# Cosine and sine products of a Fourier stage kept in separate PSUM halves, with three shared two-bank PSUM slots and mixing over whole batches

## The chip, the cores and the metric

One core of a Trainium2 chip runs the whole program. The metric is the device time of one execution in microseconds. The kernel before took 491.13, 491.68 and 493.02 us.

## The reference

The input x has 8 batches of 3072 positions of 256 channels, in f32. Two steps follow each other:

```python
X = np.fft.fft(np.fft.fft(x, axis=1), axis=2)
x = X.real                                      # (8, 3072, 256)
x_prev = x shifted by one position (first row 0)
xk = mu_k * x + (1 - mu_k) * x_prev
xr = mu_r * x + (1 - mu_r) * x_prev
k = max(xk @ w_k, 0)                            # 256 -> 1024
v = (k * k) @ w_v                               # 1024 -> 256
out = sigmoid(xr @ w_r) * v
```

## The kernel before, in words

**The Fourier part** works on one batch at a time and splits the 3072 positions into 48 x 64. It needs only real arithmetic on half of the channel pairs and half of the positions, since the real part of the result is symmetric. A GpSimd DMA loads a half batch as f16 (tile `xh`, line 101), VectorE forms sum and difference of the channel halves (`butterfly`, line 114, tile `eo`), and three kinds of matmul items follow on TensorE:
- **A items** (line 364, tile `psA`): 4 matmuls of 96 columns each, the Fourier sum over 48. ScalarE copies the result to tile `a` as f16.
- **D items** (line 397, tile `psD`): 4 matmuls of 128 columns for two units of work, the Fourier sum over the channels; ScalarE copies into `g_all`, a ring of 10 units of 384 columns.
- **C items** (lines 413, 415, 416, tile `psC`): the last sequence stage. For each of 27 slices, three matmuls with different weights: cosine table `m1` against 128 columns that are the same table twice (line 413), sine table `m2` with both signs side by side (128 columns, line 415), and `m1` once more for the second half only (64 columns, line 416). All three accumulate in PSUM, so that the two halves of a slice leave PSUM as finished rows, and ScalarE copies them to `y`.

For batch 0, `a_first` (line 381) does the butterfly inside the matmuls: two accumulating matmuls of 96 columns for each sum and each difference.

**The mixing** (`mix`, lines 456, 462, 473) is on VectorE: differences of neighbouring slices `d`, `t = mu * d` and `x = y + t` (or minus), for 8 slices at a time. The half m = 1 is the mirrored one, written backwards.

**The network part** is cut in 48 chunks of 512 positions (8 batches x 3 pieces x 2 halves) and each chunk in 4 steps. Step n has one K piece (4 matmuls of 512 columns, line 488, into a two-bank tile `psK`), its relu on ScalarE (line 492), its square on VectorE every second step (line 497), and, 5 steps late (`LAG`), one V tile (8 matmuls of 256 columns, line 518, tile `psV`). Every two steps four matmuls of line 506 make `psR`, ScalarE takes the sigmoid (line 510), VectorE multiplies (line 525), and SyncE's queue writes the output.

**PSUM** has 8 banks: `psK` two tiles of two banks, `psV` two of one bank, and `psF`, shared by the A, D, C and R items, two of one bank.

**The order** is written by hand: `work` holds for each half step the items to issue between the matmuls, and `pin_order` fixes each engine's instructions in program order. An engine that waits holds up all that stands behind it. Ahead of step 0 the program builds its tables, and batch 0 goes through A, D and C, with matmuls on zeros (`keep_busy`, line 136) in between.

## Time and profile before

| | |
|---|---|
| Median of three runs | 491.68 us (491.13 to 493.02) |
| The profiled execution's own time | 490.52 us |
| Span of its trace, first to last instruction | 488.4 us |
| Time outside the span | 2.1 us |
| TensorE busy | 469.4 us (96%) |
| ScalarE busy | 383.3 us (78%) |
| VectorE busy | 366.8 us (75%) |
| Mean granted clock of TensorE | 0.988 |

In the profile PE is TensorE's matmuls, PEld its weight loads, DVE VectorE, ACT ScalarE, POOL GpSimd and SP SyncE. A group of rows names the line of the program, the engine, the operation, what is written from what, the shape, the count, and the busy time with the mean of one in ns. Matmuls overlap each other: the mean of one is the time from its start to its last result, and what one costs in a stream is the distance between the starts of two neighbours. A row of windows names a stretch of the span, then its length and each engine's busy time in it, and TensorE's granted clock, where 1.00 is full speed.

### The profile page before, as it was taken

How to read it: one execution, taken by the hardware profiler on the slowest of the kernel's cores; microseconds unless marked ns; L12 is line 12 of the kernel's file. 1: busy time of each engine (PE TensorE's matmuls, PEld its weight loads, DVE VectorE, ACT ScalarE, POOL GpSimd, SP SyncE). 2: the span in 40 equal slices, each digit the busy share in tenths (PEclk: the TensorE clock that was granted, in tenths of full speed). 3: DMA queues.
4: the chain of work that ended last, by engine and by line, in shares of the span. 5: the costliest groups of instructions: out<-in, count | busy, mean ns of one | idle time of the engine just before them, and what ended most of it. 6: DMA issues, size and time to landing. Idle time of an engine off the chain costs nothing.

```text
span 488.4 us, 10652 instructions
## 1 busy us (share of the span) xinstructions
PE 469.4 (96%) x4325; PEld 345.5 (71%) x4325; DVE 366.8 (75%) x614; ACT 383.3 (78%) x559; POOL 38.7 (8%) x64
## 2 busy tenths in 40 slices
PE   7879889999999999999999999999999999999996
...
PEclk9889989999999999999999999999999999999999
...
GB/s 141 53 196 109 112 104 107 99 77 64 111 125 50 66 127 47 125 51 65 126 82 97 46 96 93 50 66 54 57 56 55 65 51 59 58 57 74 72 67 87
DMA packets 32565, 40.28 MB, mean 82 GB/s; under 512 B 4164, under 2 KB 30276, under 8 KB 31172
## 3 DMA queue, kind: packets, MB, share of 16 engines
...
q14 instruction: 15, 0.12, 0.1%
...
## 4 chain that ended last, share of the span: by engine, by line
PE 85%; DVE 1%; ACT 1%; issue 0%; DVEq 0%
PE psV L518 32%; PE psK L488 31%; PE psR L506 8%; PE psD L397 4%; PE psA L364 4%; PE psC L413 2%; PE psC L415 2%; PE psC L416 1%; ACT rl L492 0%; DVE o L525 0%; DVE x L473 0%; DVE t L462 0%; DVE d L456 0%; ACT a L356 0%; DVEq L525 0%
## 5 line engine op out<-in xcount | busy, mean ns | idle before, releaser
L492 ACT ACTIVATE rl<-psK 128x1024 f16<-128x1024 f32 x192 | 196.2, 1022 | 34.1 <-PE psK L488 34.1
L488 PE MATMUL psK<-x,wk 128*128 128x512 f16 x768 | 218.5, 381 | 1.7 <-DVE x L473 1.1
L518 PE MATMUL psV<-wv_sb,k 128*128 128x256 f16 x1536 | 199.3, 273 | 0.0
L518 PEld LDWEIGHTS <-k 128*128 128x128 f16 x1536 | 150.6, 98 | 38.0 <-issue 0.5
L497 DVE TENSOR_TENSOR k<-rl 128x2048 f16<-128x2048 f16 x96 | 117.5, 1224 | 25.3 <-ACT rl L492 24.9
L525 DVE SCALAR_TENSOR_TENSOR o<-psV,r 128x512 f32<-128x512 f32 x96 | 66.3, 690 | 78.2 <-PE psV L518 62.8
L488 PEld LDWEIGHTS <-wk 128*128 128x128 f16 x768 | 62.3, 98 | 22.3 <-issue 3.4
L473 DVE TENSOR_TENSOR x<-y,t 128x1024 f16<-128x1024 f16 x96 | 66.5, 693 | 3.3
L356 ACT ACTIVATE g_all<-psD 128x512 f16<-128x512 f32 x90 | 53.4, 602 | 16.6 <-PE psD L397 10.1
L356 ACT ACTIVATE a<-psA 128x384 f16<-128x384 f32 x112 | 54.9, 490 | 14.1 <-PE psA L364 8.1
L510 ACT ACTIVATE r<-psR 128x512 f16<-128x512 f32 x96 | 57.3, 597 | 2.7 <-PE psR L506 2.7
L506 PE MATMUL psR<-wr,x 128*128 128x256 f16 x384 | 57.6, 272 | 0.0
L506 PEld LDWEIGHTS <-x 128*128 128x128 f16 x384 | 37.5, 98 | 24.8 <-issue 0.5
L356 ACT ACTIVATE y<-psC 128x512 f16<-128x512 f32 (+2 forms) x52 | 30.0, 577 | 19.3 <-PE psC L416 19.3
L364 PEld LDWEIGHTS <-eo 96*128 96x128 f16 x448 | 31.5, 98 | 18.9 <-DVE eo L114 4.1
L364 PE MATMUL psA<-w_a,eo 96*128 96x96 f16 x448 | 37.7, 206 | 3.8 <-DVE eo L114 3.8
L397 PEld LDWEIGHTS <-a 128*128 128x128 f16 x384 | 28.7, 98 | 14.2 <-issue 1.0
L101 POOL DMA_DIRECT2D xh<-in_x_dram x36 | 18.6, 525 | 246.9 <-DVE eo L114 245.6
L397 PE MATMUL psD<-w_eo,a 128*128 128x128 f16 x368 | 35.6, 220 | 0.2
L415 PE MATMUL psC<-m,g_all 128*128 128x128 f16 x208 | 34.3, 221 | 1.6 <-DVE m L300 1.6
L413 PE MATMUL psC<-m,g_all 128*128 128x128 f16 x208 | 34.3, 221 | 1.5 <-ACT g_all L356 0.8
L114 DVE TENSOR_TENSOR eo<-xh 96x2048 f16<-96x2048 f16 x28 | 34.0, 1214 | 0.0
...
## 6 DMA issues: line engine op xcount, KB each, us to landing
...
wk<-in_moe_w_k_dram,row_i POOLq DMA_INDIRECT x4
wr<-in_moe_w_r_dram,row_i POOLq DMA_INDIRECT x4
mu_f<-in_moe_mu_k_dram SPq DMA_DIRECT2D x1, 0.0 KB
```

The costliest lines, as they stand in the source:

```text
L356: nc.scalar.activation(out=out_ap, in_=in_ap, func=AF.Copy)
L364: nc.tensor.matmul(out=ps[:, 96 * i:96 * i + 96], lhsT=eo[:, 4 * grp + i, e, :], rhs=w_a[0:96], start=True, stop=True)
L397: nc.tensor.matmul(out=_v(ps, 256 * i + 64 * (1 - e), [(128, 2), (1, 64)]), lhsT=a_t[b][e][:, 2 * u:2 * u + 2, :], rhs=w_eo[:, e, :], star ...
L413: nc.tensor.matmul(out=o, lhsT=g[:, 128:256], rhs=_v(m1, 64 * sl, [(0, 2), (1, 64)]), start=True, stop=False)
L473: V.tensor_tensor(out=dst, in0=_v(y, 512 * i + 192 * m, [(64 * NSL, 2), (1, 512)]), in1=t, op=ALU.subtract if m else ALU.add)
L488: nc.tensor.matmul(out=st["kp"][:, 512 * hs:512 * hs + 512], lhsT=wk_sb[m][a][:, 128 * fc:128 * fc + 128], rhs=xk[:, a, m], start=(a == 0) ...
L492: nc.scalar.activation(out=st["rl"][:, 2 * ds:2 * ds + 2], in_=st["kp"].rearrange("p (f t) -> p f t", f=2), func=AF.Relu, bias=0.0, scale= ...
L497: V.tensor_tensor(out=k2_t[c][:, 2 * ds - 2:2 * ds + 2], in0=r, in1=r, op=ALU.mult)
L506: nc.tensor.matmul(out=ps[:, 256 * h:256 * h + 256], lhsT=x_t[b, i, 1][:, a, m, 128 * tb:128 * tb + 128], rhs=wr_sb[m][a], start=(a == 0), ...
L510: nc.scalar.activation(out=st["r"], in_=ps, func=AF.Sigmoid)
L518: nc.tensor.matmul(out=st["v"][:, 256 * h:256 * h + 256], lhsT=k2_t[c][:, fc, 128 * tb:128 * tb + 128], rhs=wv_sb[:, fc], start=(fc == 0), ...
L525: V.scalar_tensor_tensor(out=o.rearrange("p a b -> p (a b)"), in0=st["v"], scalar=16.0, in1=st["r"], op0=ALU.mult, op1=ALU.mult)
```

## The change

- **C items** write the cosine product P (one matmul of 64 columns) to one bank and the sine product Q (two accumulating matmuls of 64 columns, the second with the cosine table and the third block of weights) to the other bank of a two-bank tile. Both are copied to a tile `pq`. VectorE then makes the rows: `y` = P + Q and P - Q (`halves`). The table of the sine with the other sign and its making fall away. The tables of one column (slice 25) are swapped by three small VectorE instructions.
- **PSUM**: K pieces and A, D, C and R items all take a two-bank tile from three slots `psW` in turn; V keeps two one-bank slots. So A items have 8 matmuls, D items 8 (4 units), C items 7 slices, and R items a whole chunk of 512 positions, and each is copied in one ScalarE instruction. `g_all` holds all 24 units of a batch.
- **Mixing** goes over 24 slices at once: one difference for each half, `t` (`scaled`) and `x` (`mixed`) of 1536 elements. Tiles of the mixing, `y`, `a` and `pq` have one buffer each, `xh` and `eo` two in place of three.
- **Chunks** go by half m first, then by piece i. In a step the K piece comes whole, then the items, then the V tile; the square and the output product are issued at the end of a step.
- **Start**: batch 0 and the first half of batch 1 use `a_sum`: sum and difference side by side, two accumulating matmuls of 192 columns. 9 slices of the tables are made first, then 18. Before step 0 stand 9 slices of batch 0 (12 before), 12 matmuls on zeros inside the start (18 before), and batch 0's mixing of the next slices goes into steps 0 to 9.

```diff
-    xh_pool = ctx.enter_context(tc.tile_pool(name="xh", bufs=3))
-    eo_pool = ctx.enter_context(tc.tile_pool(name="eo", bufs=3))
-    a_pool = ctx.enter_context(tc.tile_pool(name="a_sb", bufs=1))
-    y_pool = ctx.enter_context(tc.tile_pool(name="y_sb", bufs=2))
-    mix_pool = ctx.enter_context(tc.tile_pool(name="mix", bufs=2))
+    xh_pool = ctx.enter_context(tc.tile_pool(name="xh", bufs=2))
+    eo_pool = ctx.enter_context(tc.tile_pool(name="eo", bufs=2))
+    y_pool = ctx.enter_context(tc.tile_pool(name="y_sb", bufs=1))
+    mix_pool = ctx.enter_context(tc.tile_pool(name="mix", bufs=1))
-    psum = ctx.enter_context(tc.tile_pool(name="psum", bufs=8, space=bass.MemoryType.PSUM))
-    def ps_k():
-        return psum.tile([P, 1024], FP32, name="psK", tag="psK", bufs=2)
+    ps_n = {"W": 0, "V": 0}
+    def ps_slot(kind, n, cols):
+        k = ps_n[kind] % n
+        ps_n[kind] += 1
+        return psum.tile([P, cols], FP32, name=f"ps{kind}{k}", tag=f"ps{kind}{k}", bufs=1)
+    def ps_w():
+        return ps_slot("W", 3, 1024)
     def ps_v():
-        return psum.tile([P, 512], FP32, name="psV", tag="psV", bufs=2)
-    def ps_f(name):
-        return psum.tile([P, 512], FP32, name=name, tag="psF", bufs=2)
+        return ps_slot("V", 2, 512)
...
-        ps = ps_t("psA", wide)
+        ps = ps_w()
+        for i in range(8):
+            nc.tensor.matmul(out=ps[:, 128 * i:128 * i + 96], lhsT=eo[:, 8 * j + i, e, :],
+                             rhs=w_pm[0:96, 0], start=True, stop=True)
+        evac(_v(a_t[b], 3072 * e + 2 * (16 * h + 8 * j), [(64, 48), (2, 8), (1, 2)]),
+             _v(ps, 0, [(2, 48), (128, 8), (1, 2)]), eng)
+    def a_sum(b, h, q0, eng="A"):
+        if (h, q0) == (0, 0):
+            a_tile(b)
+        xh = xh_t[b, h]
+        ps = ps_w()
         for i in range(4):
-            nc.tensor.matmul(out=ps[:, 96 * i:96 * i + 96],
-                             lhsT=eo[:, 4 * grp + i, e, :], rhs=w_a[0:96],
-                             start=True, stop=True)
-        src = _v(ps, 0, [(2, 48), (96, 4), (1, 2)])
-        dst = _v(a_t[b][e], 8 * (4 * h + grp), [(64, 48), (2, 4), (1, 2)])
-        evac(dst, src, eng)
...
-    def d_item(b, up, eng="A", wide=False):
-        ps = ps_t("psD", wide)
-        for i in range(2):
-            u = 2 * up + i
+    def d_item(b, n, eng="A"):
+        ps = ps_w()
+        for i in range(4):
+            u = 4 * n + i
             for e in range(2):
                 nc.tensor.matmul(out=_v(ps, 256 * i + 64 * (1 - e), [(128, 2), (1, 64)]),
-        evac(g_of(2 * up)[:, :, 1:257], ps.rearrange("p (i c) -> p i c", i=2), eng)
+        for h in range(len(eng)):
+            c = 4 // len(eng)
+            evac(g_all[:, 4 * n + c * h:4 * n + c * h + c, 1:257],
+                 ps[:, 256 * c * h:256 * c * (h + 1)].rearrange("p (i c) -> p i c", c=256),
...
+    def c_item(b, s0, n, eng="A"):
+        if s0 == 0:
-        n = min(4, NSL - 4 * grp)
+            y_t[b, "pq"] = y_pool.tile([P, 2, NSL, 64], FP16, name="pq")
+        pq = y_t[b, "pq"]
+        ps = ps_w()
-            g = g_of(u)[:, u % 2]
-            o = ps[:, 128 * i:128 * i + 128]
-            nc.tensor.matmul(out=o, lhsT=g[:, 128:256],
-                             rhs=_v(m1, 64 * sl, [(0, 2), (1, 64)]), start=True, stop=False)
-            nc.tensor.matmul(out=o, lhsT=g[:, 0:128], rhs=m2[:, sl], start=False, stop=False)
-            nc.tensor.matmul(out=o[:, 64:128], lhsT=g[:, 256:384], rhs=m1[:, sl],
-                             start=False, stop=True)
+            sl = s0 + i
+            u = {-1: 1, 24: 0, 25: 23}.get(sl - 1, sl - 1)
+            for o, col, m, first, last in ((0, 128, m1, True, True), (512, 0, m2, True, False),
+                                           (512, 256, m1, False, True)):
+                nc.tensor.matmul(out=ps[:, o + 64 * i:o + 64 * i + 64],
+                                 lhsT=g_all[:, u, col:col + 128], rhs=m[:, sl],
+                                 start=first, stop=last)
...
+        evac(pq[:, :, s0:s0 + n, :], _v(ps, 0, [(512, 2), (64, n), (1, 64)]), eng)
+    def halves(b, lo, hi, hs=(0, 1)):
+        pq = y_t[b, "pq"]
+        for h in hs:
+            V.tensor_tensor(out=y_t[b][:, h, lo:hi], in0=pq[:, 0, lo:hi], in1=pq[:, 1, lo:hi],
+                            op=ALU.subtract if h else ALU.add)
+    def diff(b, lo, hi, hs=(0, 1)):
+        if (lo, hs[0]) == (0, 0):
+            x_t[b] = mix_pool.tile([P, 2, 26, 64], FP16, name="d")
+        y = y_t[b]
+        a0, a1 = hs[0], hs[-1] + 1
+        V.tensor_tensor(out=x_t[b][:, a0:a1, lo:hi], in0=y[:, a0:a1, lo + 1:hi + 1],
+                        in1=y[:, a0:a1, lo:hi], op=ALU.subtract)
+    def scaled(b, j, m, a, lo, hi, eng="V"):
...
+        mu = (mu_m if m else mu_f)[:, a, j:j + 1]
+        src, dst = x_t[b][:, a, 2 * m + lo:2 * m + hi], x_t["t", a][:, lo:hi]
+        if eng == "V":
+            V.tensor_scalar(out=dst, in0=src, scalar1=mu, scalar2=None, op0=ALU.mult)
...
+    def mixed(b, j, m, a, lo, hi):
+        if (a, lo) == (0, 0):
+            x_t[b, j, m] = mix_pool.tile([P, 2, 1536], FP16, name=f"x{j}{m}")
+        xo, n = x_t[b, j, m], 64 * (hi - lo)
+        dst = _v(xo, 1536 * a + 1535 - 64 * lo, [(-1, n)]) if m else (
+            xo[:, a, 64 * lo:64 * hi])
+        V.tensor_tensor(out=dst, in0=_v(y_t[b], 64 * (NSL * a + lo + 3 * m), [(1, n)]),
+                        in1=_v(x_t["t", a], 64 * lo, [(1, n)]),
+                        op=ALU.subtract if m else ALU.add)
+    def mix(b, j, m, a, lo=0, hi=24):
+        scaled(b, j, m, a, lo, hi)
+        mixed(b, j, m, a, lo, hi)
+    def mix2(b, j, m, lo, hi):
+        for a in range(2):
+            mix(b, j, m, a, lo, hi)
...
+    def k_piece(c, ds):
+        b, m, i = c
+        xk = x_t[b, 0, m]
+        if ds == 0:
+        ps = ps_w()
+        for hs in range(2):
+            fc = 2 * ds + hs
...
-            nc.tensor.matmul(out=st["kp"][:, 512 * hs:512 * hs + 512],
-                             lhsT=wk_sb[m][a][:, 128 * fc:128 * fc + 128],
-                             rhs=xk[:, a, m], start=(a == 0), stop=(a == 1))
...
+                nc.tensor.matmul(out=ps[:, 512 * hs:512 * hs + 512],
+                                 lhsT=wk_sb[m][a][:, 128 * fc:128 * fc + 128],
+                                 rhs=xk[:, a, 512 * i:512 * i + 512],
+                                 start=(a == 0), stop=(a == 1))
...
+    def square(c, ds):
+        r = st["rl"][:, 2 * ds - 2:2 * ds + 2]
+        V.tensor_tensor(out=k2_t[c][:, 2 * ds - 2:2 * ds + 2], in0=r, in1=r, op=ALU.mult)
+    def r_item(c):
+        b, m, i = c
+        ps = ps_w()
+        for tb in range(4):
...
+        st["r", c] = o_pool.tile([P, 1024], FP16, name="r", bufs=2)
...
+    a_sum(0, 0, 0)
+    a_sum(0, 0, 4)
     keep_busy(3)
-    m_wrap(0, NS1)
-    a_first(2, 0, "A")
-    m_sines(0, NS1)
-    a_first(2, 1, "V")
-    a_first(3, 0, "V")
-    m_rest(0, NS1)
-    a_first(3, 1, "A")
-    keep_busy(3)
-    d_item(0, 0, "A", True)
-    d_item(0, 1, "V", True)
-    d_item(0, 2, "A", True)
-    d_item(0, 3, "V", True)
-    c_item(0, 0, "A", True)
-    d_item(0, 4, "V", True)
-    c_item(0, 1, "A", True)
-    d_item(0, 5, "V", True)
-    mix(0, 0, 0, 0, 0, 7)
-    c_item(0, 2, "AV", True)
-    mix(0, 0, 0, 0, 7, 8)
-    keep_busy(8)
-    for a in range(2):
-        V.tensor_copy(out=mu_m[:, a], in_=mu_f[:, 1 - a])
-    V.tensor_copy(out=mu_m[0:1], in_=mu_f[0:1])
+    a_sum(0, 0, 8)
+    a_sum(0, 0, 12)
+    m_sine(0, 0, NS1)
+    m_sine(1, 0, NS1)
+    a_sum(0, 1, 0)
+    eo_sine()
+    a_sum(0, 1, 4, "V")
+    keep_busy(2)
+    a_sum(0, 1, 8, "V")
+    eo_rest()
+    a_sum(0, 1, 12)
+    m_wrap(0, NS1, NSL)
+    m_sine(0, NS1, NSL)
+    m_rest(0)
+    keep_busy(2)
+    d_item(0, 0, "AV")
+    d_item(0, 1, "AV")
+    m_wrap(1, NS1, NSL)
+    c_item(0, 0, 5)
+    halves(0, 0, 5)
+    c_item(0, 5, 4, "AV")
+    m_sine(1, NS1, NSL)
+    d_item(0, 2)
+    halves(0, 5, 9)
+    diff(0, 0, 8)
+    d_item(0, 3, "AV")
+    mix2(0, 0, 0, 0, 8)
+    keep_busy(5)
...
+    chunks = [(b, m, i) for b in range(B) for m in range(2) for i in range(3)]
+    for n, c in enumerate(chunks):
+        at(4 * n + 4, r_item, c)
+    at(0, d_item, 0, 4)
+    at(0, mix2, 0, 1, 0, 0, 8)
+    at(1, m_rest, 1)
+    at(1, c_item, 0, 9, 8)
+    at(1, d_item, 0, 5, "V")
+    at(2, a_sum, 1, 0, 0)
+    at(2, halves, 0, 9, 17)
+    at(2, diff, 0, 8, 16)
+    at(3, c_item, 0, 17, 8)
+    at(3, a_sum, 1, 0, 4, "V")
+    at(3, mix2, 0, 0, 0, 8, 16)
+    at(4, a_sum, 1, 0, 8)
+    at(4, halves, 0, 17, 25)
+    at(5, c_item, 0, 25, 2)
+    at(5, a_sum, 1, 0, 12)
+    at(5, diff, 0, 16, 24)
...
+    at(6, mix2, 0, 0, 0, 16, 24)
+    at(5, butterfly, 1, 1, 0)
+    at(7, butterfly, 1, 1, 1)
...
+    at(9, halves, 0, 25, 27)
+    at(9, diff, 0, 24, 26)
+    at(9, mix2, 0, 1, 0, 16, 24)
+    for n, st0 in enumerate((7, 8, 9, 10)):
+        at(st0, a_item, 1, 1, n // 2, n % 2, "A")
+    for n, st0 in enumerate((12, 13, 13, 14, 15, 17)):
+        at(st0, d_item, 1, n)
+    for n, st0 in enumerate((14, 15, 18, 19)):
+        at(st0, c_item, 1, (0, 7, 14, 21)[n], 7 if n < 3 else 6)
+        for n, st0 in enumerate((2, 4, 6, 8) if b else (9, 10, 12, 14)):
+            at(s0 + st0, mix, b, n // 2, 1, n % 2)
+                at(s0 + 12 + 2 * h, load_xh, b + 3, h)
+        t = b + 2
+        if t < B:
+            for n, st0 in enumerate((9, 10, 12, 14)):
+                at(s0 + st0, butterfly, t, n // 2, n % 2)
+            for n, st0 in enumerate((18, 19, 21, 22, 23, 25, 26, 27)):
+                at(s0 + st0, a_item, t, n // 4, n // 2 % 2, n % 2)
+            for n, st0 in enumerate((29, 30, 31, 34, 35, 38)):
+                at(s0 + st0, d_item, t, n)
+            for n, st0 in enumerate((33, 37, 39, 41)):
+                at(s0 + st0, c_item, t, (0, 7, 14, 21)[n], 7 if n < 3 else 6)
+        t = b + 1
+        if t < B:
+            at(s0 + 16, halves, t, 0, 14)
+            at(s0 + (18 if b else 20), halves, t, 14, 27)
+            at(s0 + (19 if b else 20), diff, t, 0, 26, (0,))
+            at(s0 + (20 if b else 21), diff, t, 0, 26, (1,))
+            at(s0 + 21, mix, t, 0, 0, 0)
+            at(s0 + 22, mix, t, 0, 0, 1)
+            at(s0 + 24, mix, t, 1, 0, 0)
+            at(s0 + 25, mix, t, 1, 0, 1)
...
-            c, ds = chunks[step // 4], step % 4
-            k_half(c, ds, 0, kst)
-            due(step, 0)
-            k_half(c, ds, 1, kst)
+            k_piece(chunks[step // 4], step % 4)
+        due(step, "x")
         vs = step - LAG
         if vs >= 0:
-            cv, tb = chunks[vs // 4], vs % 4
-            if tb % 2 == 0:
-                r_pair(cv, tb // 2, vst)
-            v_tile(cv, tb, vst)
-        due(step, 1)
+            v_tile(chunks[vs // 4], vs % 4)
+        due(step, "w")
+        if vs >= 0 and vs % 2:
+            v_out(chunks[vs // 4], vs % 4)
+        if step < nk and step % 2:
+            square(chunks[step // 4], step % 4)
```

**TensorE at one slice of a C item.** Before:

```order
L413 LDWEIGHTS g_all_205
L413 MATMUL psC_1111<-m1_211,g_all_205 128x128
L415 LDWEIGHTS g_all_205
L415 MATMUL psC_1111<-m2_212,g_all_205 128x128
L416 LDWEIGHTS g_all_205
L416 MATMUL psC_1111<-m1_211,g_all_205 128x64
```

and now:

```order
L407 LDWEIGHTS g_all_189
L407 MATMUL psW0_3139<-m1_195,g_all_189 128x64
L407 LDWEIGHTS g_all_189
L407 MATMUL psW0_3139<-m2_196,g_all_189 128x64
L407 LDWEIGHTS g_all_189
L407 MATMUL psW0_3139<-m1_195,g_all_189 128x64
```

`m1` and `m2` are the cosine and sine tables. The 128-column matmuls are gone; each of the three has 64 columns and still its own weights.

**ScalarE inside a batch, at R items.** Before, with D and C items (`g_all`, `y`), and then now, with A items (`a`), whose turn it is there:

```order
L492 ACTIVATE rl_1983<-psK_2027 128x1024
L510 ACTIVATE r_2039<-psR_2034 128x512
L356 ACTIVATE g_all_205<-psD_2051 128x2x256
L356 ACTIVATE g_all_205<-psD_2060 128x2x256
L492 ACTIVATE rl_1983<-psK_2057 128x1024
L356 ACTIVATE y_1771<-psC_2085 128x2x256
```

```order
L485 ACTIVATE rl_2093<-psW2_2094 128x1024
L503 ACTIVATE r_2109<-psW0_2100 128x1024
L485 ACTIVATE rl_2093<-psW1_2127 128x1024
L348 ACTIVATE a_1920<-psW2_2133 128x48x16
L485 ACTIVATE rl_2093<-psW0_2156 128x1024
L348 ACTIVATE a_1920<-psW1_2162 128x48x16
```

Every copy now frees one of three slots `psW0` to `psW2` in turn, and the relu of a K piece stands in the same turn as the other copies; copies are fewer and twice as long.

**VectorE in steps 1 to 3**, up to the x that the second chunk's K piece of step 4 reads (`x0` written a second time before, `x00` now). Before:

```order
L354 CAST g_all_205<-psD_559 128x2x256
L497 TENSOR_TENSOR k2_536<-rl_535 128x2048
L291 TENSOR_SCALAR m1_211<-m1_211 64x64
L291 TENSOR_SCALAR m2_212<-m2_212 64x64
L298 MEMSET m1_211 64x32
L299 MEMSET m2_212 64x32
L300 TENSOR_SCALAR m2_212<-m2_212 128x15x64
L462 TENSOR_SCALAR t_576<-d_490,mu_f_91 128x512 x2
L473 TENSOR_TENSOR x1_579<-y_449,t_576 128x2x512
L462 TENSOR_SCALAR t_587<-d_490,mu_m_92 128x512 x2
L473 TENSOR_TENSOR x0_513<-y_449,t_587 128x2x512
```

and now:

```order
L286 MEMSET m2_196 64x32
L491 TENSOR_TENSOR k2_444<-rl_445 128x2048
L424 TENSOR_TENSOR y_365<-pq_366 128x512 x2
L432 TENSOR_TENSOR d_414<-y_365 128x2x512
L346 CAST a_525<-psW2_571 128x96x8
L444 TENSOR_SCALAR t0_581<-d_414,mu_f_88 128x512
L457 TENSOR_TENSOR x00_429<-y_365,t0_581 128x512
L444 TENSOR_SCALAR t1_584<-d_414,mu_f_88 128x512
L457 TENSOR_TENSOR x00_429<-y_365,t1_584 128x512
```

Two sums (`y` from `pq`), a difference and a copy of `a` stand ahead of that x, where the making of the sine table's other sign and the mixing for the other network stood.

356 lines of the change are left out of this document (116 added, 240 removed).

## The prediction

> **What bounds the kernel now.** I read the page's shares and slices first, then windows by stage, then TensorE's own timeline for what each matmul costs in a stream.
>
> ```profile
> PE 469.4 (96%) x4325; PEld 345.5 (71%) x4325; DVE 366.8 (75%) x614; ACT 383.3 (78%) x559; POOL 38.7 (8%) x64
> ...
> PE   7879889999999999999999999999999999999996
> ...
> PEclk9889989999999999999999999999999999999999
> ```
>
> ```profile
> 15.87:19.28 3.41, 3.26 (x34) 2.81 (x34) 2.17 (x9) 2.25 (x4) 3.26 (x7) 0.50 0.00 0
> 94.09:150.30 56.21, 56.21 (x532) 42.08 (x530) 43.97 (x68) 47.92 (x72) 2.02 (x4) 1.00 0.45 96
> ```
>
> The window of one whole batch (24 steps, 56.21 us) has TensorE busy for all of it, ScalarE for 47.9 and VectorE for 44.0. But matmuls overlap, so a busy TensorE need not be at its peak. The timeline inside a batch tells what it does there:
>
> ```profile
> 250.72 0.22 PE L413 MATMUL psC<-m,g_all 128*128 128x128 f16 x1
> 250.77 0.22 PE L415 MATMUL psC<-m,g_all 128*128 128x128 f16 x1
> 250.83 0.19 PE L416 MATMUL psC<-m,g_all 128*128 128x64 f16 x1
> 250.86 0.22 PE L413 MATMUL psC<-m,g_all 128*128 128x128 f16 x1
> ...
> 251.28 1.03 PE L488 MATMUL psK<-x,wk 128*128 128x512 f16 x4
> 252.15 0.60 PE L506 MATMUL psR<-wr,x 128*128 128x256 f16 x4
> 252.58 1.04 PE L518 MATMUL psV<-wv_sb,k 128*128 128x256 f16 x8
> 253.46 0.39 PE L397 MATMUL psD<-w_eo,a 128*128 128x128 f16 x4
> 253.68 0.59 PE L488 MATMUL psK<-x,wk 128*128 128x512 f16 x2
> ...
> 209.02 0.34 PE L364 MATMUL psA<-w_a,eo 96*128 96x96 f16 x4
> 209.19 0.60 PE L488 MATMUL psK<-x,wk 128*128 128x512 f16 x2
> ```
>
> Distances between starts: 4 K matmuls in 0.87 us (216 ns each), 4 R in 0.43 and 8 V in 0.88 (109 ns), 4 D in 0.22 (56), 4 A in 0.17 (42). A slice of C takes 250.72 to 250.86, 0.14 us: 56 + 56 + 28.5. Every price is near its columns: 512, 256, 128, 96, 64. Sum over a batch: 96 K x 0.216 + 192 V x 0.109 + 48 R x 0.109 + 64 A x 0.042 + 48 D x 0.056 + 27 slices x 0.1405 = 20.7 + 20.9 + 5.2 + 2.7 + 2.7 + 3.8 = 56.0 us of the 56.21. So in the steady batches TensorE streams columns with no gap, and only fewer columns make it faster. What it loses, it loses at the start (the digits 7 and 8; PEclk dips in three slices, and where I looked closer, from 15.87 us, it is 0.50 for 3.41 us).
>
> **The loss at the start, as a sum.** Where step 0 begins and where the program ends:
>
> ```profile
> 26.37 0.59 PE L488 MATMUL psK<-x,wk 128*128 128x512 f16 x2 [0.98 <-DVE x L473]
> ...
> 482.83 0.82 PE L518 MATMUL psV<-wv_sb,k 128*128 128x256 f16 x6
> ```
>
> From step 0 on there are 768 K, 1536 V, 384 R, 448 A, 360 D matmuls and 204 slices: 165.9 + 167.4 + 41.9 + 18.8 + 20.2 + 28.7 = 442.9 us. The last matmul starts at 482.83 + 5 x 0.109 = 483.4. So 483.4 - 26.4 - 442.9 = 14.1 us are lost after step 0, nearly all in the first two batches. The end takes 488.4 - 483.4 = 5.0 us, and the profiled execution 490.52 - 488.4 = 2.1 us beyond its span.
>
> **The change part by part: TensorE.** C: a slice has three matmuls of 64 columns in place of 128 + 128 + 64. The row of 250.83 gives 28.5 ns for one such, with new weights behind it, so 3 x 28.5 = 86 ns, and 55 ns less for each slice: 207 slices after the new step 0 cost 17.7 us where 204 cost 28.7. A matmul of 192 columns is in no row; between 84 ns (two of 96) and 109 (one of 256) it lies by its columns at 83 to 84: the first half of batch 1 is 32 x 0.084 = 2.7 us, where 32 of 96 columns cost 1.3. The other A matmuls are 416 x 0.042 = 17.5, D 352 x 0.056 = 19.7. K, V and R stay. From step 0: 165.9 + 167.4 + 41.9 + 2.7 + 17.5 + 19.7 + 17.7 = **432.8 us, 10.1 less**.
>
> Can weights be loaded each 28.5 ns in a row of such matmuls?
>
> ```profile
> 250.83 0.10 PEld L413 LDWEIGHTS <-g_all 128*128 128x128 f16 x1
> 250.86 0.10 PEld L415 LDWEIGHTS <-g_all 128*128 128x128 f16 x1
> ```
>
> A load lasts 98 ns, but two stand 28 ns apart here and A's 42 apart in a row, so loads overlap. A sustained row at 28 is not in the trace. Bounds: 28.5 and A's 42 ns. I take 28.5, since the load behind each 64-column matmul already fits; at 42 C costs 621 x 13.5 ns = 8.4 us more.
>
> The Trainium skill speaks against such short matmuls. "TensorE: Matmul & The Clock Gate", section "Back-to-back issue gap", gives about 81 ns for each pair of load and 128-column matmul in a real kernel. By that figure as a floor, C would cost an estimated 621 x 81 ns = 50 us, and the change would lose. The trace disagrees: 56 ns for 128 columns with a load each, and 42 for 96.
>
> **ScalarE and VectorE in a steady batch.** These cover the rest, if they stay under TensorE.
>
> ```profile
> L492 ACT ACTIVATE rl<-psK 128x1024 f16<-128x1024 f32 x192 | 196.2, 1022 | 34.1 <-PE psK L488 34.1
> L510 ACT ACTIVATE r<-psR 128x512 f16<-128x512 f32 x96 | 57.3, 597 | 2.7 <-PE psR L506 2.7
> ...
> L356 ACT ACTIVATE a<-psK 128x768 f16<-128x768 f32 x6 | 4.8, 809 | 8.0 <-PE psK L381 6.2 <-remote 1.8
> ```
>
> ```profile
> L497 DVE TENSOR_TENSOR k<-rl 128x2048 f16<-128x2048 f16 x96 | 117.5, 1224 | 25.3 <-ACT rl L492 24.9
> L473 DVE TENSOR_TENSOR x<-y,t 128x1024 f16<-128x1024 f16 x96 | 66.5, 693 | 3.3
> L525 DVE SCALAR_TENSOR_TENSOR o<-psV,r 128x512 f32<-128x512 f32 x96 | 66.3, 690 | 78.2 <-PE psV L518 62.8 <-issue 8.7 <-ACT rl L492 4.1
> L114 DVE TENSOR_TENSOR eo<-xh 96x2048 f16<-96x2048 f16 x28 | 34.0, 1214 | 0.0
> L462 DVE TENSOR_SCALAR t<-d,mu_m 128x512 f16<-128x512 f16 x96 | 29.3, 347 | 0.0
> ...
> L456 DVE TENSOR_TENSOR d<-y 128x896 f16<-128x896 f16 x1 | 0.6, 615 | 0.0
> ```
>
> ScalarE: 24 relu, 6 R and 6 D of 1024 at 1.02, 8 A at 0.81, 4 C of 768 to 896 at about 0.9: 24.5 + 6.1 + 6.1 + 6.5 + 3.6 = 46.8 us a batch, in a batch of 56.0 - 27 x 0.055 = 54.5. VectorE: 12 squares, 12 outputs and 4 butterflies stay (14.7 + 8.3 + 4.9). New are 4 sums of 832 to 896 (0.6 each, 2.4 us), added work that lies beside TensorE. The mixing shrinks: 8 t of 1536 at 0.61 (0.347 plus 1024 more at the slope of its row), 8 x of 1536 at 0.95 and 2 differences of 1664 at 1.0 make 14.5, where 24 t, 12 x and 3 differences cost 8.3 + 8.3 + about 2.2. Sum 44.8. Both stay below 54.5; with that cover gone, each us over would be a us of the batch.
>
> The slots: a third tile later comes the same slot. Steady steps hold at most a K piece and one item. The tightest turn is K, A item, V, K, A item: from the end of the first K to the second A item lie 0.34 + 0.87 + 0.86 = 2.07 us, and the copy of K needs 1.0 and its start. Nothing waits there, and the relu's wait for TensorE (34.1 us in its row) shows ScalarE early. V's square has a whole step more. I cost the slots at nothing; 0.1 us on each of 48 tiles would be 4.8 us a batch.
>
> **The start.** Up to step 0:
>
> ```profile
> 18.78 0.81 ACT L356 ACTIVATE a<-psK 128x768 f16<-128x768 f32 x1 [1.16 <-PE psK L381]
> ...
> L510 ACT ACT_TABLE_LOAD x1 | 1.3, 1283 | 0.0
> L282 ACT ACTIVATE m<-rl,m_pi 128x960 f16<-128x960 int32 x1 | 1.1, 1116 | 0.0
> ```
>
> The A stage ends on the landing of x, which is loaded in the same order, so the last copy of `a` ends at 18.5 to 19.6 again. Then ScalarE has the sine of 18 slices (1.3), two half D copies (0.6 each) and the first C copy (0.7): 22.2. VectorE follows with two sums (0.7), a half C copy (0.4), two sums (0.6), the difference (0.7), a half D copy (0.7, as the output's 0.69 for 512 from PSUM), t and x for both halves (0.35 + 0.43, twice 1.6): 26.9 at the middle. I take step 0 at **27.0** (26 to 29), 0.6 later.
>
> After it VectorE leads. Step 4's x stands behind: the copy of the fifth D item (about 3.4 to 4.6 us after step 0), seven small table rows (1.0), a square (1.2), two sums and a difference (1.5), a copy of `a` (768 from PSUM, 0.96 by the same slope), t and x (1.6): 11 us, against TensorE's 7.0 of steps 0 to 3. So 4.0 lost. Then R's first sigmoid loads its table (1.3) ahead of the relu of step 5, and the item behind waits for a slot: 1.8. Step 12 reads the first mirrored x; VectorE has by then 1.6 + 1.6 for mixing, butterfly 1.2 and square 1.2 ahead of it, and comes some 3.3 after TensorE. Sum 9.1. Each long wait can bring a stretch at half clock, 1.7 us each; partly these fall into waits. With 2.4 for that: **11.5** (6 to 16) where 14.1 were lost; the second batch's items are spread more thinly.
>
> The half clock by the skill's same page, section "Part 1: The HAM clock gate": after an idle window of about 3.4 us the clock is halved. The trace agrees on the length (3.41 us at 0.50 in the window quoted), though TensorE was not idle for all of the stretch before it.
>
> Loads: on POOL's queue the load of batch 1 now waits for the A matmuls of batch 0, and later weights queue behind it; they are needed ten us and more after, so I cost it at nothing.
>
> **Sum:** 27.0 + 432.8 + 11.5 + 5.0 = 476.3, and 2.1 outside is 478.4 in the profiled execution's terms (490.52). The median of runs is 1.2 above that execution; I say **479 us**.
>
> **The rivals.** *Weight loads set C's pitch* (42 ns): +8.4, so 487. For it: no long row at 28 in the trace. Against: single pairs at 28. Chance 0.08. With 12.7 us gained in all, 28.5 + 12,700 / 621 = 49 ns is the point from which there is no gain; at the 98 ns that a load lasts, C costs 43 us more and the kernel 522: 0.03. *The start is no shorter*: the VectorE chain is longer by its small rows and the half clock falls on work: 29 + 432.8 + 16 + 5.0 + 2.1 = 485; 0.17. *ScalarE holds TensorE through the shared slots* (slower than before): the relu now stands in one turn with every item, so a late copy stops the next K piece, and K stops all. It decides from 12.7 us over 7 x 48 tiles, 38 ns a tile; at 0.1 us it costs 33 us, so 512. Against: 2.07 us between, and ScalarE at 86%. 0.05. *The start is clean*: 26 + 432.8 + 6 + 5 + 2.1 = 472; 0.12. My forecast: 0.55.
>
> **How the numbers follow.** Range 472 to 487: bounds of start and waits, with C at 42 ns at the top. A measurement of this kernel tells about 0.5% from no change (489.2 to 494.1). Slower is the slot rival and half of loads at 98 ns and more, 0.07; same 0.05, from the upper ends of start and pitch; faster 0.88.
>
> **What would show it.** Right: starts of the 64-column matmuls 28 to 29 ns apart, a batch of 54.5 us with TensorE busy throughout, step 0 near 27 and step 4 some 11 us later with a wait for x. Wrong: a C slice over 0.1 us, K pieces waiting for copies by ScalarE, or gaps beyond the second batch.

## The result, and the profile after

The changed kernel takes **479.38 us** (median of four executions, 477.65 to 480.65) where the kernel before takes 492.26 on the same chip. The ratio is 0.9738, with a 95% interval from 0.9693 to 0.9783. 479.0 had been forecast. The profiled execution took 480.65 us, its span 478.9.

The page of the changed kernel, busy times, then TensorE and its clock by fortieths of the span:

```profile
PE 458.6 (96%) x4255; PEld 335.8 (70%) x4255; DVE 360.2 (75%) x493; ACT 357.8 (75%) x389; POOL 36.8 (8%) x59
...
PE   7776989999999999999999999999999999999996
...
PEclk9978989999999999999999999999999999999999
```

From the seventh fortieth (72 us) to the last but one every digit of TensorE is a 9, as before. The windows show one whole batch, and then the stretches in which the clock is halved (columns: window, length, busy time with count of PE, PEld, DVE, ACT and POOL, granted clock, DMA share, GB/s):

```profile
95.34:150.05 54.71, 54.71 (x531) 40.64 (x529) 43.09 (x51) 44.34 (x50) 2.01 (x4) 1.00 0.41 88
...
9.60:13.01 3.41, 3.41 (x21) 2.86 (x19) 3.11 (x9) 1.56 (x3) 3.41 (x4) 0.50 0.52 98
26.66:33.49 6.83, 5.94 (x43) 3.54 (x44) 2.79 (x8) 3.01 (x4) 2.48 (x3) 0.50 1.14 190
40.32:43.73 3.41, 2.94 (x10) 1.32 (x11) 3.34 (x7) 0.80 (x1) 0.00 (x0) 0.50 0.00 0
64.21:67.62 3.41, 3.41 (x22) 2.59 (x20) 3.38 (x5) 2.34 (x3) 1.00 (x2) 0.50 0.49 60
```

A batch takes 54.71 us (56.21 before), TensorE is busy for all of it, VectorE for 43.1 and ScalarE for 44.3. TensorE's timeline, the places in which it waited, one C item in a steady batch (171.54) and the end (start, length, line, shape, count, and in brackets the idle time before and who ended it):

```profile
7.90 1.49 PE L374 MATMUL psW<-w_pm,xh 96*128 96x192 f16 x16 [1.83 <-DVE w_pm L214]
...
27.51 2.06 PE L481 MATMUL psW<-x,wk 128*128 128x512 f16 x4 [3.48 <-DVE x L457]
...
40.68 2.16 PE L481 MATMUL psW<-x,wk 128*128 128x512 f16 x4 [2.96 <-DVE x L457]
...
46.34 0.34 PE L407 MATMUL psW<-m,g_all 128*128 128x64 f16 x6 [0.60 <-ACT r L503]
47.05 0.82 PE L374 MATMUL psW<-w_pm,xh 96*128 96x192 f16 x8 [0.37 <-ACT a L348]
...
61.24 0.38 PE L481 MATMUL psW<-x,wk 128*128 128x512 f16 x1
63.64 0.92 PE L481 MATMUL psW<-x,wk 128*128 128x512 f16 x3 [2.02 <-DVE x L457]
...
171.54 0.78 PE L407 MATMUL psW<-m,g_all 128*128 128x64 f16 x21
172.15 1.04 PE L510 MATMUL psV<-wv_sb,k 128*128 128x256 f16 x8
...
469.79 4.42 PE L510 MATMUL psV<-wv_sb,k 128*128 128x256 f16 x39
```

The C item of seven slices starts 21 matmuls of 64 columns in 172.15 - 171.54 = 0.61 us: 29 ns each, 87 ns a slice, where a slice had cost 141. Step 0 starts at 27.51, step 4 at 40.68. The last matmul starts at 469.79 + 38 x 0.109 = 473.93.

### The profile page after: what moved, and what is told of

It is laid out like the page before. It is cut to its first block, busy times and chain, and to the rows that moved or that the text cites. A ratio compares the mean times of both kernels' runs of the same rounds, so it can differ in the third digit from the quotient of the medians.

```text
span 478.9 us, 10061 instructions
## 1 busy us (share of the span) xinstructions
PE 458.6 (96%) x4255; PEld 335.8 (70%) x4255; DVE 360.2 (75%) x493; ACT 357.8 (75%) x389; POOL 36.8 (8%) x59
## 4 chain that ended last, share of the span: by engine, by line
PE 90%; DVE 6%; ACT 2%; issue 1%; POOL 0%; POOLq 0%; DVEq 0%; ACTq 0%
PE psV L510 35%; PE psW L481 34%; PE psW L498 9%; PE psW L386 5%; PE psW L407 4%; PE psW L360 4%; DVE x L457 1%; DVE t L444 1%; DVE a L346 1%; DVE w_pm L212 1%; DVE g_all L346 1%; DVE k L491 0%; ACT g_all L348 0%; DVE o L518 0%; DVE g_all L246 0%
## 5 line engine op out<-in xcount | busy, mean ns | idle before, releaser
L485 ACT ACTIVATE rl<-psW 128x1024 f16<-128x1024 f32 x192 | 196.5, 1023 | 99.2 <-PE psW L481 99.2
L481 PE MATMUL psW<-x,wk 128*128 128x512 f16 x768 | 200.3, 383 | 8.6 <-DVE x L457 8.5
L457 DVE TENSOR_TENSOR x<-y,t 128x1536 f16<-128x1536 f16 (+1 forms) x72 | 62.6, 870 | 2.5
L348 ACT ACTIVATE a<-psW 128x768 f16<-128x768 f32 x61 | 49.1, 807 | 6.3 <-PE psW L374 6.3
L498 PE MATMUL psW<-wr,x 128*128 128x256 f16 x384 | 51.2, 278 | 0.0
L503 ACT ACTIVATE r<-psW 128x1024 f16<-128x1024 f32 x48 | 48.9, 1018 | 1.5 <-PE psW L498 1.5
L348 ACT ACTIVATE g_all<-psW 128x1024 f16<-128x1024 f32 (+1 forms) x47 | 46.7, 1001 | 1.0 <-PE psW L386 1.0
L386 PE MATMUL psW<-w_eo,a 128*128 128x128 f16 x384 | 29.8, 223 | 0.5 <-DVE rl L266 0.5
L348 ACT ACTIVATE pq<-psW 128x896 f16<-128x896 f32 (+4 forms) x33 | 28.4, 861 | 1.8 <-PE psW L407 0.9
L360 PE MATMUL psW<-w_pm,eo 96*128 96x96 f16 x416 | 26.3, 205 | 0.0
```

The costliest lines, as they stand in the source:

```text
L348: nc.scalar.activation(out=out_ap, in_=in_ap, func=AF.Copy)
L360: nc.tensor.matmul(out=ps[:, 128 * i:128 * i + 96], lhsT=eo[:, 8 * j + i, e, :], rhs=w_pm[0:96, 0], start=True, stop=True)
L386: nc.tensor.matmul(out=_v(ps, 256 * i + 64 * (1 - e), [(128, 2), (1, 64)]), lhsT=a_t[b][:, e, 2 * u:2 * u + 2, :], rhs=w_eo[:, e, :], star ...
L457: V.tensor_tensor(out=dst, in0=_v(y_t[b], 64 * (NSL * a + lo + 3 * m), [(1, n)]), in1=_v(x_t["t", a], 64 * lo, [(1, n)]), op=ALU.subtract ...
L481: nc.tensor.matmul(out=ps[:, 512 * hs:512 * hs + 512], lhsT=wk_sb[m][a][:, 128 * fc:128 * fc + 128], rhs=xk[:, a, 512 * i:512 * i + 512], ...
L485: nc.scalar.activation(out=st["rl"][:, 2 * ds:2 * ds + 2], in_=ps.rearrange("p (f t) -> p f t", f=2), func=AF.Relu, bias=0.0, scale=0.25)
```

## The experiments

They ran on several chips. The kernel before took 486 to 488 us on two of them and mostly 490 to 494 on the others, so ratios, each with the kernel before on the same chip, and the stages of the traces are compared rather than bare times. For that the changed kernel itself was run again as well.

### The changed kernel on another chip

> The changed kernel once more, beside the kernel before, to have it on one chip with the experiments: the kernel before took 486.6 there and not 492.3. Theory (the gain is in the steady batches, 1.50 us each, and does not depend on the chip; what differs between chips is the start of either kernel): steady batches 54.71 again; from step 0 to the last matmul 432.8 us of streaming again; the ratio anywhere between 0.970 and 0.985, by how many half-clock stretches each start gets. Rival (the ratio 0.9738 holds on any chip): 0.970 to 0.978.

477.8 us against 487.8: ratio 0.9797 (0.9754 to 0.9840). Steady batches of 54.71 us again. The rows of step 0, step 4 and step 12:

```profile
26.77 0.38 PE L481 MATMUL psW<-x,wk 128*128 128x512 f16 x1 [2.69 <-DVE x L457]
...
39.00 0.39 PE L481 MATMUL psW<-x,wk 128*128 128x512 f16 x1 [2.79 <-DVE x L457]
...
61.34 1.35 PE L481 MATMUL psW<-x,wk 128*128 128x512 f16 x3 [2.02 <-DVE x L457]
```

The same three waits, but only two half-clock stretches (from 27.3 and 61.5 us) where the first profile had five. The changed kernel differs by 1.6 us between the chips, the kernel before by 4.5. The theory fits: step 24, where the steady batches begin, comes at 95.34 and 93.05 us in the two profiles and came at 94.09 before, so the start as a whole is not shown to be better, and the gain lies in the batches. The intervals of the two ratios overlap, so the rival (one ratio on any chip) is not ruled out by them.

### C alone, undone and done

```diff
 # the changed kernel, C summed in PSUM again
+            nc.tensor.matmul(out=o, lhsT=g_all[:, u, 128:256],
+                             rhs=_v(m1, 64 * sl, [(0, 2), (1, 64)]), start=True, stop=False)
+            nc.tensor.matmul(out=o, lhsT=g_all[:, u, 0:128], rhs=m2s[:, sl],
+                             start=False, stop=False)
+            nc.tensor.matmul(out=o[:, 64:128], lhsT=g_all[:, u, 256:384], rhs=m1[:, sl], ...)
...
```

The table of the sine with the other sign is made again, VectorE's sums fall away, and `y` gets two buffers.

> The changed kernel with one part undone: the last stage sums in PSUM again, with 128 + 128 + 64 columns a slice and the coefficients with both signs; the three W slots, the merged copies and the whole-batch mix stay. Theory (the gain is TensorE's columns): a slice costs 141 ns in place of 86, 216 slices x 55 ns = 11.9 us more, of which 207 lie after step 0 (11.4); a steady batch takes 54.71 + 27 x 0.055 = 56.2 us; the time is 490 to 492, so nothing of the gain is left. VectorE loses four sums a batch (43.1 to about 40.7 us) and that moves nothing. Rival (slots, merged copies and the mix over whole batches carry part of the gain): the batch stays below 55.7 us and the time at or below 485.

```diff
 # the kernel before, C's products apart in the halves of its one-bank tile
+            for o, col, m, first, last in ((0, 128, m1[:, sl], True, True),
+                                           (256, 0, m2[:, sl, 0], True, False),
+                                           (256, 256, m1[:, sl], False, True)):
+                nc.tensor.matmul(out=ps[:, o + 64 * i:o + 64 * i + 64], lhsT=g[:, col:col + 128],
+                                 rhs=m, start=first, stop=last)
...
+            V.tensor_tensor(out=y_t[b][:, h, lo:hi], in0=pq[:, 0, lo:hi], in1=pq[:, 1, lo:hi],
+                            op=ALU.subtract if h else ALU.add)
```

> The kernel before with this one part alone: three 64-column matmuls a slice, the two products copied apart and added and subtracted on VectorE; slots, small copies and small mixes as before. Theory: TensorE has 204 x 55 ns = 11.2 us less after step 0, a steady batch goes from 56.21 to 54.7 us; VectorE goes from 44.0 to about 48 us a batch, still under TensorE; the time is 480 to 483. Rival (the small pieces make VectorE too long or too late once the sums are added, and the mix over whole batches was needed for the gain): gaps of TensorE in steady batches, 0.5 to 1.5 us a batch, and 485 or more.

Undone: 484.96 us, ratio 0.9961 (0.9945 to 0.9976). Done alone: 476.6 us, ratio 0.9805 (0.9759 to 0.9850). Both ran on one chip, with the kernel before at 486.62. One batch of each, first the one undone:

```profile
90.67:146.82 56.15, 56.15 (x532) 42.06 (x530) 41.05 (x47) 44.56 (x50) 2.01 (x4) 1.00 0.42 85
```

```profile
86.64:141.56 54.92, 54.92 (x532) 40.71 (x530) 47.15 (x86) 47.92 (x72) 2.56 (x5) 1.00 0.50 102
```

With C summed in PSUM the batch is back at 56.15 us although slots, copies and mixing are the new ones. With C alone split it is 54.92, VectorE at 47.2 and ScalarE at 47.9. C's split alone reaches the ratio of the whole change within the intervals, and 0.21 us a batch is all that it lacks in the stream. The rest of the change is worth 0.4% by itself. I had put the time of the first at 490 to 492, from the other chip, and its loss at 11.9 us. Beside the changed kernel's ratio of 0.9797 its ratio says 0.0164 x 487 = 8.0 us (0.9738 would say 10.9); the batches account for six times 1.44, 8.6 us. So the batches came as worked out; the 3 us more that I had put down for the slices of the first batch do not show, and as TensorE waits in that batch anyway, its waits may hide them.

With C alone split, which keeps the old start, step 0 came at 22.98 us and step 24 at 86.63, without a half-clock stretch; the changed kernel has 26.77 and 93.05 in its better profile. How much of that is the old start, and how much the chip and the execution, was not tried.

### Two slots in place of three

```diff
-        return ps_slot("W", 3, 1024)
+        return ps_slot("W", 2, 1024)
```

> The changed kernel with two W slots in place of three: it measures the slack of the slots. Theory (2.07 us between a tile's end and the next use of its slot with three slots is well above the copy of 1.0 us; with two only V, 0.87, and an item of 0.22 to 0.43 lie between): with two slots TensorE waits some 0.1 to 0.5 us for ScalarE at each of the 27 steps a batch that have an item, 3 to 13 us a batch, so 500 to 580 in all. Rival (copies follow so fast that even two slots suffice): within 2 us of 479, and the third slot does nothing.

486.75 us, ratio 1.0009 (0.9986 to 1.0032). Neither expectation held. A steady batch, and TensorE's groups with the idle time ahead of them:

```profile
98.75:153.94 55.19, 55.19 (x530) 40.56 (x529) 43.00 (x52) 44.35 (x49) 2.00 (x4) 1.00 0.41 87
```

```profile
L386 PE MATMUL psW<-w_eo,a 128*128 128x128 f16 x384 | 29.8, 222 | 2.0 <-ACT rl L485 1.3 <-ACT a L348 0.5 <-ACT pq L348 0.3
L360 PE MATMUL psW<-w_pm,eo 96*128 96x96 f16 x416 | 26.3, 206 | 1.3 <-ACT rl L485 1.3
L407 PE MATMUL psW<-m,g_all 128*128 128x64 f16 x648 | 24.2, 193 | 3.2 <-DVE g_all L346 1.8 <-ACT rl L485 1.3
```

A steady batch loses only 0.48 us, 20 ns at each of its 24 items (8 A, 6 D, 4 C, 6 R; the 27 that I had written are its slices), not 0.1 to 0.5 us. Items now wait for the relu (`rl`), 6.2 us in all, and every wait that the trace lists is in the first batch, which takes 71.8 us where the changed kernel's took 67.8 and 66.3 in its two profiles. The waits stand in steps 1 and 3, where TensorE has no V tile yet, and at the second item of steps that hold two (5, 8, 12 to 15, 18, 19); steady batches have one item to a step. So the third slot earns some 4 to 5.5 us in the first batch and 0.5 in each later one, and with three slots the copies hold nobody in a steady batch.

### Mixing in pieces again

```diff
-        scaled(b, j, m, a, lo, hi)
-        mixed(b, j, m, a, lo, hi)
+        for q in range(lo, hi, 8):
+            scaled(b, j, m, a, q, q + 8)
+            mixed(b, j, m, a, q, q + 8)
```

> The changed kernel with each mix of a whole batch made in three pieces of 8 slices again. VectorE gets 16 more scalings and 16 more additions a batch: (3 x 0.347 - 0.61) x 8 + (3 x 0.43 - 0.95) x 8 = 6.2 us, 43.1 becomes about 49 of the 54.7 us of TensorE. Theory that VectorE's order has room: the batch stays at 54.7 us, the time within 1.5 us of 479, and the mix over whole batches is worth nothing to the end. Rival (the mix comes just before the steps that read it, so VectorE's backlog at steps 21 to 26 shows): TensorE waits for x at steps 24 and 28, 1 to 3 us a batch, and the time is 486 to 500.

483.45 us, ratio 0.9931 (0.9907 to 0.9954): between the two. Two batches:

```profile
92.71:148.32 55.61, 55.04 (x532) 40.60 (x529) 48.86 (x85) 44.35 (x50) 2.01 (x4) 1.00 0.40 86
148.32:203.03 54.71, 54.71 (x532) 40.61 (x529) 47.99 (x83) 44.35 (x50) 2.02 (x4) 1.00 0.40 88
```

VectorE is busy for 48.0 to 48.9 us, and the steady batches stay at 54.71. What the trace shows of the loss is 0.9 us in the second batch and 3.0 after step 168 (55.0 us from there to the last matmul, against 52.05): the last batch has no A, D and C items, TensorE is quicker there, and V waits for VectorE's square and output. That is 3.9 of the 6.5 us between the two ratios; the first batch shows 0.8 more, and the rest stays open. Mixing over whole batches is cover for those places, not a gain of the steady batch.

### The start: the table, and zeros where TensorE waits

```diff
-    nc.gpsimd.iota(kcol_i, pattern=[[1, NSL], [48, 64]], base=-1, channel_multiplier=0)
+    nc.gpsimd.iota(kcol_i[:, 0:NS1], pattern=[[1, NS1], [48, 64]], base=-1, ...)
 # ahead of the second angles
+    nc.gpsimd.iota(kcol_i[:, NS1:NSL], pattern=[[1, NSL - NS1], [48, 64]], base=NS1 - 1, ...)
```

> The changed kernel with the table of column numbers written by GpSimd in two pieces again, 9 slices at first and the other 18 just before the second set of angles. Theory (VectorE's two small products for w_pm, 2.66 and 2.53 us in place of 0.74 and 0.61, last as long as GpSimd's table of 1728 columns beside them): they take 0.5 to 0.9 us, the first A matmul starts at about 6.1 us in place of 7.9, the half clock near 9.6 is gone, step 0 comes 1 to 2.5 us sooner and the time falls by as much. Rival (the A stage is bound by its own matmuls and copies, or the later table delays the second sine): step 0 within 0.5 us of that of the changed kernel, no change of time.

```diff
-    keep_busy(5)
+    keep_busy(20)
+    at(3, keep_busy, 13)
```

> The changed kernel with more matmuls on zeros where TensorE waits: 20 in place of 5 before step 0 (3.2 us more) and 13 more (2.8 us) at the end of step 3, where K of step 4 waits for x. Theory (the half clock follows idle TensorE and falls on work): the half-clock stretches from 26.7 to 33.5 and from 40.3 to 43.7 us are gone; at half clock TensorE does 1.7 us less work in each, of which part falls into waits, so 2 to 4 us less in all. Rival (VectorE and ScalarE set the pace of steps 0 to 12, and half clock only fills waits): under 1 us.

Table in two: 474.8 us, ratio 0.9751 (0.9702 to 0.9800). Zeros: 475.57 us, ratio 0.9758 (0.9726 to 0.9790). Against 477.8 on the same chip that is 3.0 and 2.2 us less; the intervals of the ratios overlap, so it is the traces that must carry these two. VectorE and GpSimd in the changed kernel, and below with the table in two:

```profile
4.93 2.66 DVE L212 TENSOR_SCALAR w_pm<-t,lo 128x48 f16<-128x48 f32 x1 [0.18 <-ACT t L204]
...
5.86 1.68 POOL L157 IOTA kcol_i<- 128x1728 int32 x1
```

```profile
4.93 0.26 DVE L213 TENSOR_SCALAR w_pm<-t,lo 128x48 f16<-128x48 f32 x1 [0.18 <-ACT t L205]
...
5.86 0.66 POOL L157 IOTA kcol_i<- 128x576 int32 x1
...
5.81 1.48 PE L377 MATMUL psW<-w_pm,xh 96*128 96x192 f16 x16 [0.71 <-DVE pos_l L217]
...
24.34 2.07 PE L484 MATMUL psW<-x,wk 128*128 128x512 f16 x4 [2.69 <-DVE x L460]
```

The product that makes the first weights ends at 7.59 beside the long table (which ends at 7.54) and at 5.19 beside the short one. The first A matmul moves from 7.90 to 5.81, and step 0 from 26.77 to 24.34. With zeros, step 0 came at 27.4, and from there to step 4 passed 10.6 us in place of 12.2; no half clock fell there, though it stood from 20.2 to 23.6 and from 61.2 to 64.6. The changed kernel's profile on this chip has two stretches as well, at other places (27.3 and 61.5). So the trace shows a shorter way to step 4, but it does not show that the zeros won the 2.2 us, rather than the places at which the stretches fell in these executions.

### A start in another order

```diff
 # with the table in two
-    d_item(0, 0, "AV")
-    d_item(0, 1, "AV")
+    d_item(0, 0, "V")
+    d_item(0, 1)
...
-    c_item(0, 5, 4, "AV")
-    m_sine(1, NS1, NSL)
+    c_item(0, 5, 4, "V")
...
-    d_item(0, 3, "AV")
+    d_item(0, 3)
...
-    keep_busy(5)
+    m_sine(1, NS1, NSL)          # behind the mixing
+    keep_busy(9)
...
-    at(1, m_rest, 1)
+    at(4, m_rest, 1)
...
-    at(1, d_item, 0, 5, "V")
+    at(1, d_item, 0, 5)
...
-    at(3, a_sum, 1, 0, 4, "V")
+    at(3, a_sum, 1, 0, 4)
```

> The changed kernel with the table in two pieces and VectorE freed ahead of the two x that TensorE waits for: D items 0 and 1 copied whole, one by VectorE and one by ScalarE, in place of halves one behind the other; D item 3 wholly by ScalarE; the second C piece wholly by VectorE; the second sine of the coefficients behind D item 3; in steps 0 to 3 the copy of D item 5 and one of `a` by ScalarE, and the small rows of the table moved from step 1 to step 4. Theory (VectorE's chain sets step 0 and step 4, as the prediction said of step 4): step 0 at 23 to 25 us, step 4 no more than 11 us behind it, last matmul 3 to 6 us sooner, ratio about 0.965. Rival (ScalarE becomes the late one in steps 0 to 4, with 10.6 us of copies and relu there): step 0 sooner, but step 8 as late as in the changed kernel, and under 1.5 us gained.

**471.15 us**, ratio 0.9658 (0.9622 to 0.9695), 6.65 less than the changed kernel on the same chip. Step 0, step 4 and step 12:

```profile
22.84 0.38 PE L484 MATMUL psW<-x,wk 128*128 128x512 f16 x1 [0.81 <-DVE x L460]
...
31.91 1.02 PE L484 MATMUL psW<-x,wk 128*128 128x512 f16 x4
...
51.69 0.38 PE L484 MATMUL psW<-x,wk 128*128 128x512 f16 x1
54.09 1.43 PE L484 MATMUL psW<-x,wk 128*128 128x512 f16 x3 [2.02 <-DVE x L460]
```

Step 0 comes 3.9 us sooner, step 4 without a wait 9.1 us behind it, and step 8 at 42.84 us in place of 50.09; the last matmul gains the same 7.25 us. The rival (ScalarE late, step 8 no sooner) falls. For step 4 the traces show VectorE's chain: in the changed kernel's first profile VectorE works without a gap from 34.00 us to that step's x at 40.6, and 3.2 us of this (a copy of `g_all`, the small rows, a copy of `a`) are what the edit moves away. Ahead of step 0 the edit also moves a sine on ScalarE back and adds four matmuls on zeros, and its parts were not timed apart. What is left is step 12, and one half-clock stretch behind it.

The next kernel moves the butterflies of batch 2 away from there:

```diff
-            for n, st0 in enumerate((9, 10, 12, 14)):
+            for n, st0 in enumerate((9, 10, 12, 14) if b else (13, 14, 15, 17)):
```

> The kernel with the table in two pieces and the start reordered, and one thing more: the four butterflies of batch 2 (1.21 us each on VectorE) at steps 13, 14, 15 and 17 in place of 9, 10, 12 and 14. In the run without this, VectorE was busy from 38.4 us on without a gap, K of step 12 waited 2.02 us for the second mirrored x, and a half-clock stretch from 54.2 to 57.6 us followed. Theory (the x of step 12 is late because two butterflies stand ahead of it on VectorE, 2.4 us): the wait at step 12 is below 0.3 us, the half clock there is gone, step 24 comes 3 to 4 us sooner, and the ratio falls from 0.966 to about 0.958. Rival (the butterflies only push what VectorE has to do in steps 16 to 24, and the wait comes back at step 24): step 24 sooner by under 1.5 us.

470.47 us, ratio 0.9550 (0.9526 to 0.9574), but on a chip with the kernel before at 492.9. Step 12 still waited 0.89 us, a half-clock stretch came at 40.6 us, ahead of it, and step 24 came at 86.66 us, no sooner than the 85.80 of the kernel without; where 3 to 4 us sooner had been expected. Both ran once more on one chip, with the kernel before at 491.27:

> The reordered start once more, on one chip with the next kernel, since the two had been timed on chips on which the kernel before differs by 5 us. Theory (the two executions of the next kernel's profile differ from this one only at step 12): step 12 waits 2 us for the mirrored x and a half-clock stretch follows. Rival: none beyond that the wait comes out otherwise in another execution.

> The butterflies of batch 2 later, beside the reordered start on the same chip. Theory (2.8 us that the first profile shows between steps 8 and 24 stay to the end): 1.5 to 3 us less than the reordered start on the same chip. Rival (what is won at step 12 is lost to another half-clock stretch before, as from 40.6 to 44.0 us in the first profile): the same within 1 us.

473.12 us without and **471.31** with the later butterflies (ratios 0.9610, 0.9558 to 0.9663, and 0.9582, 0.9535 to 0.9629). The wait at step 12, first without:

```profile
58.53 0.81 PE L484 MATMUL psW<-x,wk 128*128 128x512 f16 x3 [2.02 <-DVE x L460]
```

```profile
55.97 0.81 PE L484 MATMUL psW<-x,wk 128*128 128x512 f16 x3 [0.89 <-DVE x L460]
```

The wait falls by 1.1 us, less than the 1.7 that I had expected, and 1.8 us of time is within what the intervals allow for none. From step 12 to step 24 pass 31.31 us in both profiles with the later butterflies, 34.11 and 32.45 without. No half clock followed step 12 in the second profile without; it came from 40.7 us there, so that expectation failed in part. Step 0 came at 24.97 us in this profile and not at 22.84: an A item waited for the landing of x until 10.07 us, in the first until 8.81. By their ratios both are well ahead of the changed kernel and of the one before.

### How often weights can be loaded

```diff
+    def short_row(n):
+        ps = ps_w()
+        for i in range(96):
+            nc.tensor.matmul(out=ps[:, (64 * i) % 1024:(64 * i) % 1024 + n],
+                             lhsT=wv_sb[:, i % 8, 0:128], rhs=zeros[:, 0:n], ...)
+    for st0, n in ((60, 64), (64, 48), (68, 32), (72, 16)):
+        at(st0, short_row, n)
```

> The changed kernel with four rows of 96 matmuls added, each with weights of its own (the weights of V in turn) and zeros as the moving side: 64 columns at step 60, 48 at step 64, 32 at step 68, 16 at step 72; nothing reads them. It measures what the prediction left between two bounds: how often weights can be loaded. Theory of the prediction (columns set the pitch, 64 at 28 to 29 ns): 29 ns at 64, and below that the columns go on, 21, 14 and 7 ns. Rival (a load of 128 x 128 weights has a pitch of its own that 64 columns just cover): 64, 48, 32 and 16 columns all stand some 26 to 29 ns apart, so that a cut below 64 columns would win nothing.

Each row, and the K matmul that follows it:

```profile
176.98 2.96 PE L618 MATMUL psW<-zeros,wv_sb 128*128 128x64 f16 x96
179.78 0.59 PE L481 MATMUL psW<-x,wk 128*128 128x512 f16 x2
...
189.27 2.56 PE L618 MATMUL psW<-zeros,wv_sb 128*128 128x48 f16 x96
191.67 0.59 PE L481 MATMUL psW<-x,wk 128*128 128x512 f16 x2
...
200.70 2.56 PE L618 MATMUL psW<-zeros,wv_sb 128*128 128x32 f16 x96
203.11 0.59 PE L481 MATMUL psW<-x,wk 128*128 128x512 f16 x2
...
211.96 2.55 PE L618 MATMUL psW<-zeros,wv_sb 128*128 128x16 f16 x96
214.36 0.81 PE L481 MATMUL psW<-x,wk 128*128 128x512 f16 x3
```

96 matmuls of 64 columns take 2.80 us, 29 ns each. With 48, 32 and 16 columns they take 2.40, 2.41 and 2.40: 25 ns each, however few the columns. So the theory (21, 14 and 7 ns) fails below 64 columns and the rival nearly holds: there is a floor, 64 columns stand 4 ns above it, and a cut to 48 would win only those. Whether the load or the matmul itself sets it, these rows do not tell. The Trainium skill, "TensorE: Matmul & The Clock Gate", section "Wait — 56ns, not 53.3ns?", states that starts never come closer than about 25 ns; this trace agrees.

## Why the prediction was right

**TensorE streams columns: right.** A batch had been put at 54.5 us and takes 54.71; it falls by 1.50 us for 27 x 0.055 = 1.49 worked out. The pitch of 28.5 ns, taken from one pair of rows, is 29 in a long row. The rival in which loads set 42 ns or more falls; but a floor of 25 ns lies only 4 ns below what 64 columns cost, which the prediction could not know. The pair of 81 ns that the Trainium skill, "TensorE: Matmul & The Clock Gate", gives for 128 columns in section "Back-to-back issue gap" is not seen here: 128 columns cost 56 ns, 64 cost 29.

**ScalarE, VectorE and the slots: right.** VectorE 43.1 for 44.8 worked out, ScalarE 44.3 for 46.8; no gap in a steady batch. That slots cost nothing rested on 2.07 us between uses of a slot; the run with two slots shows that they would have cost 0.5 us a batch even so, and that the slack matters in the first batch.

**The start: right in its sum, one step wrong.** Step 0 was put at 27.0 and came at 27.51 and 26.77. The A stage, put at 18.5 to 19.6, ended at 17.57 in the first profile and at 18.73 in the second, though its first matmul waited for the long table in both. The first C copy, put at 22.2, ended at 22.15 in the first; so the steps from the A stage to it took 4.6 us where 2.6 to 3.7 were worked out, and those from it to step 0 took 5.4 for 4.8. One reason is that I had put the halves of each "AV" copy side by side:

```profile
16.76 0.81 ACT L348 ACTIVATE a<-psW 128x768 f16<-128x768 f32 x1 [0.59 <-PE psW L374]
...
19.68 1.09 ACT L348 ACTIVATE g_all<-psW 128x512 f16<-128x512 f32 x2 [0.97 <-PE psW L386]
...
22.98 0.38 ACT L348 ACTIVATE pq<-psW 128x256 f16<-128x256 f32 x1 [0.83 <-PE psW L386]
...
24.41 1.50 ACT L348 ACTIVATE g_all<-psW 128x1024 f16<-128x1024 f32 x2
...
20.31 1.29 DVE L346 CAST g_all<-psW 128x512 f16<-128x512 f32 x2 [2.23 <-ACT g_all L348]
...
23.40 0.42 DVE L346 CAST pq<-psW 128x256 f16<-128x256 f32 x1 [0.54 <-ACT pq L348]
...
25.95 0.69 DVE L346 CAST g_all<-psW 128x512 f16<-128x512 f32 x1 [0.87 <-ACT g_all L348]
```

VectorE's half starts when ScalarE's is done, each time, and its row names ScalarE's half as what it waited for. The reordered start does away with this, with the long table and with other work ahead of the two x; the share of each was not taken apart.

**The waits after step 0: 11.5 worked out, 473.93 - 27.51 - 432.8 = 13.6 measured (12.1 in the second profile).** The places were right, the sizes not. Step 4 waited 2.96 us and not 4.0, the table load for the sigmoid cost 0.60 + 0.37 and not 1.8, step 12 waited 2.0 and not 3.3: 6.0 where 9.1 stood. The half clock, put at 2.4, was under-sized: after step 0, TensorE was busy in half-clock windows for about 12.3 us in that execution (5.94, 2.94 and 3.41 in the rows above), so half of that, an estimated 6.1 us, was lost. And the prices of the stream make 54.5 us a batch where 54.71 were measured; over the 432.8 us, some eight batches, that is 1.6 us more which is no wait at all. 6.0 + 6.1 + 1.6 = 13.7 accounts for the 13.6 measured; 9.1 + 2.4 = 11.5 came near it because the errors went both ways.

**The tail** is 5.0 us again, and 1.75 us lie outside the span where 2.1 were taken. GpSimd's loads cost nothing, as assumed; its table did, and that was no term of the sum at all.

That the median lies within 0.4 us of the forecast is in part luck: the four executions spread over 3.0 us, the terms after step 0 missed by 3.1 us one way and 5.3 the other, and the forecast's own 478.4 + 1.2 is 479.6 and not 479.
